# New order tables for an interleaved RWKV-6 attention and exact-GELU MLP

## The chip, the cores and the metric

The kernel runs on one core of one Trainium2 chip. The metric is the device time of one execution in microseconds, as the median of several runs. A profile is one further execution, recorded by the hardware profiler; its span is the time from its first to its last instruction.

## What is computed

An RWKV-6 attention with a recurrent state feeds an MLP with an exact GELU:

```python
# r, k, v, w: (4, 8, 768, 48), u: (8, 48)
for t in range(S):
    cur = einsum('bhd,bhe->bhde', u * k[t], v[t])
    y[t] = einsum('bhd,bhde->bhe', r[t], state + cur)
    state = w[t][..., None] * state + einsum('bhd,bhe->bhde', k[t], v[t])
x = y.transpose(0, 2, 1, 3).reshape(3072, 384)
h = x @ w_in                                   # (384, 2048)
g = 0.5 * h * (1.0 + erf(h / sqrt(2)))
out = g @ w_out                                # (2048, 384)
```

## The kernel before

The 3072 tokens are cut into 8 tiles of 384. For each tile there is an attention, `attention(x, unit)`, which leaves its result in `xT`, and an MLP, `mlp(x)`. Both are Python generators: each `next` emits the instructions of one small step. The instructions of an engine run in the order in which they are emitted, so the order of the steps is the schedule.

That order is written out by hand in two tables.

`PLAN[x]` has one character for each step of stage x. In stage 0 "." and "s" are the two units (halves of the heads) of the attention of tile 0, "l" a transfer of raw weights or of the second tile's data, "c" a step of the conversion of the weights, "f" a step of the next tile's attention, "w" the load of the next tile's v. In stages 1 to 7 "." is a step of the MLP of tile x - 1, "s" a step of the attention of tile x, "f" a step of the attention of tile x + 1, "l" a transfer for tile x + 1, "x" one of five sums of `xT` that the MLP needs (`sums_of_x`, L1029), "c" again the conversion (stage 1), "w" masks and sums of weights (stages 1 and 2). What is left of a stream when the characters end is emitted after them, save "f" (and "c" in stage 0), whose stream goes on in the next stage. The MLP of the last tile stands alone at the end.

`ORDER[x]` gives the steps of the MLP of tile x, for x from 1 on (tile 0 has a plain MLP: 16 blocks of 128 features, three products and a Gelu each, then the products with `w_out`). A letter and a digit is a step of the first half: capital letters A to G are products on TensorE, small letters mostly copies and Gelus on ScalarE. "+" is a sum on VectorE, "=" a product of the second half, "<" and "!" open and read out a bank of PSUM. The products use fewer multiplications than the plain form, with sums of blocks in their place.

The attention of tile 0 is the only work of stage 0. Each of its units makes diagonal products, then for six levels of block length a burst of products (L550), a scaling (L592, L603) and a copy by mask or by rows (L615, L612); then the transposed k (L787, L789), the state products (L817), the chain of states (L838, L833), the products with v (L859), fences that read the end of each bank (L869, L871), the products with the state (L906), and the copies into `xT` (L913, L929), part of it by way of `ysb` and transfers (L932, L936). Two warm-up matmuls (L324) stand behind most bursts. Loads in stage 0 are gated: a one-element memset on VectorE (L259, L303) stands ahead of each, so that the transfer can't be issued before VectorE has come to that place.

From tile 2 on, the attention has finer steps ("quarters": bursts L689 and L680, copies L723, L705 and L773, scalings L745, L752, L756, layouts L656, L662, L664). A weight arrives as 64-bit floats; three ScalarE operations (L432, L433, L435) and two VectorE operations (L440, L443) convert a piece of it.

Of the kernel before, what the change touches and what calls it, by code (L numbers as in the profile page):

```python
# [37 lines left out]
HALFWAY = 2  # L38
PLAN = {
    0: (  # L40
        "lllll.lll.lll.l.s.s.ssssss..sc.sssl.s.lcl.s.s.s.s..lcls.ssc.s.c.s.s.cs..cscss.s.sfwf."
    ),
    1: (
        "s.ccc.csc..cc.c.scc.scc....wscccc.c.ccsccs...cws.cccl.slclcs.cs..lslccc...ccsc...scccs.c...c.ccslwcc"
        "css..cslcc.csc.ccsccl.slc.sl...ccc.....w..f.....wfwf..wwwf..wf..xwf...wf.x.wff.f.x..ffxxw."
    ),
    2: (
        "w..s.s.slws.wws..wsw.ss.ss..s..ss.s.s.s...wl.ss......wss..s.s.sws..s.....s.ss.sws.ssw.sw..s.wss.sw.s"
        "ss.ss.w.ws.s.......s.l..ss.w....w....s.l..w.w.....sss.ll.....s....s.s...s..sss.ss.s.....ls......lls."
        ".......f.s.f..f.f....fxx....flx..x.x"  # L50
    ),
    3: (
        "s..s.............s.....s.s..ss..ss..sss..s...s.s...sssssss.s.s.l.....sssl.s..sss..s....s...ss...sss."
        ".s.sss.ss...s..s....l.....s.sls.s.....s.....s...s.ssss.s.s.l.slss....ss....s....l.ss....s.sl...lfs.."
        "...f.l....ffxx..xxx."
    ),
    4: (
        "......ss...s.......ll...s...s.s..l.......s..sls...ss.ss...s.sss.sss.sss..sss..s...s.s....ss.ssss...."
        ".ss..lss..s.sss...s...s.sl...ss..sss..s.ss.s..s.ss.......s.sss.s.s.s.........s.....s...l.ss.ls....l."
        "sfs...f..f.xxl...x.xx"  # L60
    ),
    5: (
        "s..s.s.......s..s..s....s.......s..s........sss..s...sss....sl.ss.sss.sssss....s...ss.sss...s....s.."
        "s.ls..sl.s.ss.s.s.s.s.s...s..s..s.s.s.sls.s.ssllsss.s.....sss.s..........s..s.........ss..s.llss..l."
        ".ss.f...f.f..fxx.xxl.fx."
    ),
    6: (
        "s..l...sl....s..ss................ss......sssls.s.....sl...sss.s.ssss.ss..s.s....ss...sss..ss...s..s"
        "....s...ss.s.ss.ssss.....l.ss....s..ss..s...s.s....s....sssss.sss.ss.....l......s.ss...ssls.l...l.fs"
        "..s.f...f..ff.xxf.xf.lfffffxx"  # L70
    ),
    7: (
        "........................ss.s...ss...s.ssss..s..ss.s..s......s...sss..ss....s..ss.ssss.s..ss..ssss..."
        ".s.s...ss...s.s..........s..s.s.ss.ss..s.s........s..s..s...ss.ss.s..ss.....ss.s.s......x.x...x..x.x"
    ),
}

# [19 lines left out]
W_ORDER = "empsiclratkdjfnbohqg"  # L97
ORDER = {
# [5 lines left out]
    ),  # L104
# [5 lines left out]
    ),  # L110
# [5 lines left out]
    ),  # L116
# [5 lines left out]
    ),  # L122
# [5 lines left out]
    ),  # L128
# [5 lines left out]
    ),  # L134
# [1187 lines left out]
```

## Time and profile before

| what | value |
|---|---|
| runs | 584.16, 584.63, 587.84 us; median 584.63 |
| the profiled execution, its own time | 587.29 us |
| its span | 585.5 us |
| TensorE (PE) busy | 566.6 us (97%) |
| VectorE (DVE) busy | 451.5 us (77%) |
| ScalarE (ACT) busy | 290.7 us (50%) |
| GpSimd (POOL) busy | 58.9 us (10%) |
| mean granted clock of TensorE | 0.997 |
| bytes moved | 55.07 MB, mean 94 GB/s |

How to read it: a row of the timeline has the start and length in us, the engine, the line of the kernel, the operation, what it writes and reads, how many instructions were merged, and in brackets how long the engine was idle before and what ended that. PEld is TensorE's loading of weights, which overlaps its products. SPq and ACTq are transfers issued by SyncE and ScalarE. The chain is the work that ended last, followed back step by step; "issue" in it, or in brackets, is time in which an engine waited for nothing that the profile shows. A product of 32-bit numbers leaves two records.

### The profile page before, as it was taken

To read this page: it belongs to the slowest core of one execution; us is meant where nothing else is said; L and a number is where in the kernel's file an instruction comes from. 1 tells how busy PE (TensorE), PEld (TensorE's weight loads), DVE (VectorE), ACT (ScalarE), POOL (GpSimd) and SP (SyncE) were. 2 spreads that over 40 slices of the span, in tenths; PEclk is the share of its full clock that TensorE was granted. 3 is DMA by queue.
4 is the path that set the end of the run, shared out by engine and by line. 5 is a ranking of instruction groups with operands and counts; after the bars stand their busy time and mean duration, and the time that the engine had idled before them with its cause. 6 is when DMAs were issued, how large, how long until landed. Compare 5 with 4: busy or idle time off the path is not lost.

```text
span 585.5 us, 17564 instructions
## 1 busy us (share of the span) xinstructions
PE 566.6 (97%) x7544; PEld 510.5 (87%) x7544; DVE 451.5 (77%) x880; ACT 290.7 (50%) x634; POOL 58.9 (10%) x63
## 2 busy tenths in 40 slices
PE   6879999999999999999999999989999999999997
PEld 3566667669999999999999999979999999999997
DVE  5879867998999977798897979789797988830171
ACT  2457997224852357335672367225571456525520
POOL 3100000003100111003100120002200031002200
PEclk9989999999999999999999999999999999999999
DMA  8538951123450523636222622525413242203401
GB/s 303 191 93 278 355 178 58 52 76 42 54 156 12 137 37 45 152 106 139 39 42 61 169 30 29 130 77 153 57 28 88 79 70 29 44 12 67 55 1 40
DMA packets 61853, 55.07 MB, mean 94 GB/s; under 512 B 32336, under 2 KB 46928, under 8 KB 61776
## 3 DMA queue, kind: packets, MB, share of 16 engines
q1 hardware_dynamic: 50256, 45.62, 25.5%
q0 software_dynamic: 11424, 8.26, 10.8%
q8 instruction: 59, 0.97, 0.7%
q14 instruction: 18, 0.15, 0.1%
q10 hardware_dynamic: 96, 0.07, 0.1%
HBM read 36.24 MB, written 4.72 MB: 70 GB/s over the span
## 4 chain that ended last, share of the span: by engine, by line
PE 90%; DVE 3%; issue 2%; DMA 2%; ACT 1%; SPq 1%; ACTq 0%; DVEq 0%
PE u_ps L1043 31%; PE h_ps L1043 19%; PE o_ps L1043 13%; PE h_ps L1121 5%; PE o_ps L1133 5%; PE d L689 5%; PE d L550 3%; PE y_ps L859 2%; PE y_ps L906 2%; PE kv_ps L817 2%; DMA xT<-ysb 1%; PE warm L324 1%; SPq L936 1%; DMA rkw<-in_rkw_dram 1%; DVE tot_sb L508 1%
## 5 line engine op out<-in xcount | busy, mean ns | idle before, releaser
L1043 PE MATMUL h_ps<-xT,w_in_sb 128*128 128x192 f32 x560 | 110.1, 329 | 1.4 <-DVE xT L1029 1.3
L1081 POOL DMA_DIRECT2D g<-o_sb x42 | 50.9, 1293 | 480.1 <-ACT o_sb L1076 336.4
L1043 PEld LDWEIGHTS h_ps<-xT,w_in_sb 128*128 128x128 f32 x560 | 93.2, 190 | 4.2 <-DVE xT L1029 1.9
L705 ACT COPY a_sb<-d 32x320 f32<-32x320 f32 (+5 forms) x108 | 39.1, 362 | 6.6 <-PE d L689 4.9
L1043 PE MATMUL u_ps<-s,w_in_sb 128*128 128x192 f32 x224 | 41.4, 328 | 0.0
L1043 PE MATMUL u_ps<-w_out_sb,g 128*128 128x192 f32 x224 | 41.3, 328 | 0.0
L1043 PE MATMUL o_ps<-t,g 128*128 128x192 f32 x224 | 40.6, 327 | 0.0
L1043 PEld LDWEIGHTS o_ps<-t,g 128*128 128x128 f32 x224 | 36.9, 190 | 0.5 <-ACT o_sb L1076 0.3
L1043 PEld LDWEIGHTS u_ps<-s,w_in_sb 128*128 128x128 f32 x224 | 36.9, 190 | 0.5
L1043 PEld LDWEIGHTS u_ps<-w_out_sb,g 128*128 128x128 f32 x224 | 36.9, 190 | 0.3
L723 DVE COPY_PREDICATED a_sb<-quarter,d 128x480 f32<-128x480 uint8 (+5 forms) x54 | 23.1, 438 | 12.9 <-PE d L689 11.7
L1121 PE MATMUL h_ps<-xT,w_in_sb 128*128 128x384 f32 x96 | 32.3, 491 | 0.3 <-ACT xT L913 0.3
L1133 PE MATMUL o_ps<-w_out_sb,g 128*128 128x384 f32 x96 | 32.4, 491 | 0.0
L1091 ACT COPY u_ps<-h_ps 128x384 f32<-128x384 f32 x28 | 13.1, 467 | 36.5 <-PE h_ps L1043 36.1
L550 PEld LDWEIGHTS d<-rkw 64*64 64x64 f32 x1152 | 19.6, 136 | 13.1 <-issue 7.5
L1043 PE MATMUL u_ps<-w_extra,g 128*128 128x192 f32 x168 | 30.7, 327 | 0.3 <-ACT u_ps L1167 0.3
L833 DVE SCALAR_TENSOR_TENSOR st<-st,tot_sb,kv_ps 128x48 f32<-128x48 f32 x160 | 29.4, 257 | 1.4 <-PE kv_ps L817 1.3
L932 ACT COPY ysb<-y_ps 128x384 f32<-128x384 f32 x8 | 3.8, 480 | 53.7 <-PE y_ps L906 42.9
L1072 ACT ACTIVATE g<-g 128x384 f32<-128x384 f32 x56 | 28.4, 522 | 3.6 <-DMA g<-o_sb 2.5
L689 PE MATMUL d<-kx,rkw 64*64 64x96 f32 x1152 | 29.4, 247 | 0.0
L1188 ACT ACTIVATE o_sb<-u_ps 128x192 f32<-128x192 f32 x21 | 6.9, 330 | 45.2 <-PE u_ps L1043 45.0
L1083 DVE TENSOR_TENSOR g<-g,o_sb 128x384 f32<-128x384 f32 x14 | 7.6, 554 | 28.0 <-ACT o_sb L1076 28.0
(163 smaller groups left out, 1234.5 us busy)
## 6 DMA issues: line engine op xcount, KB each, us to landing
rkw<-in_rkw_dram SPq DMA_DIRECT2D x54, 256.0 KB, 3.5
g<-o_sb POOLq DMA_DIRECT2D x42, 192.0 KB, 3.6
raw<-in_w_out_dram SPq DMA_DIRECT2D x8, 768.0 KB, 6.1
v_in<-in_v_dram SPq DMA_DIRECT2D x8, 584.0 KB, 3.9
raw<-in_w_in_dram SPq DMA_DIRECT2D x5, 768.0 KB, 8.3
rkw<-kx SPq DMA_DIRECT2D x72, 48.0 KB, 2.0
out_dram<-o_sb SPq DMA_DIRECT2D x17, 192.0 KB, 1.9
rkw<-in_rkw_dram SPq DMA_DIRECT2D x6, 384.0 KB, 6.7
```

Of the source, the lines that this page charges most:

```text
L550: nc.tensor.matmul(d[half[p], g, n * width:(n + 1) * width], lhsT=kc[half[g], b, i, p], rhs=right(half[g], b, i, p), start=True, stop=True)
L689: nc.tensor.matmul(o[half[p], i * 3 * C // 2:(i + 1) * 3 * C // 2], lhsT=kc[half[g], n // NI, n % NI, p], rhs=rx[half[g], 2 * n + p], star ...
L705: nc.scalar.copy(out=at[z, g, first:behind, (a + 1) * h:], in_=d[z, :, :, to] if g == slice(None) else d[z, :, to])
L723: nc.vector.copy_predicated(out=an[:, :, :, :, (a + 1) * h:], mask=mask.to_broadcast(data.shape), data=data)
L817: nc.tensor.matmul(kv_ps[half[g], p, i * D:(i + 1) * D], lhsT=k_t(b, i, p, g), rhs=vs(b, i, g)[half[p], 0:D], start=True, stop=True)
L833: nc.vector.scalar_tensor_tensor(out=stq[:, q, c], in0=stq[:, q, c - 1] if c else b4[:, q, NC - 1], scalar=totq[:, q, c:c + 1], in1=kvs[q ...
L1043: nc.tensor.matmul(o, lhsT=lhsT, rhs=rhs, start=start, stop=True, skip_group_check=True)
L1072: nc.scalar.activation(out=g_of(q, a, b), in_=z, func=AF.Gelu)
L1081: nc.gpsimd.dma_start(out=o, in_=z, accum_op=ALU.add)
L1091: nc.scalar.copy(out=u_of[q], in_=a_of[q])
L1121: nc.tensor.matmul(h_ps, lhsT=w_in_sb[:, f // FI, j, f % FI * 128:(f % FI + 1) * 128], rhs=xT[:, j, :], start=(j == 0), stop=(j == NJ - 1))
L1133: nc.tensor.matmul(o, lhsT=gs[f // FG][:, f % FG, i * 128:(i + 1) * 128], rhs=w_out_sb[:, f, :], start=(f == 0), stop=(f == NF - 1))
```

## The change

Only the two tables change. The table of stage 0 is replaced by one with the same steps in another order (the order that it had in the kernel ahead of the finer attention steps). The tables of stages 1 to 7, and the orders of the MLPs of tiles 1 to 6, are replaced by new ones; that of the MLP of tile 7 stays. The instructions are the same ones, and the numbers of steps of the next tile's attention that stand in a stage ("f") change from 12, 6, 4, 3, 5, 12 to 17, 9, 3, 3, 4, 12 in stages 1 to 6. The core of it, in which "..." marks what is left out:

```diff
 PLAN = {
     0: (
-        "lllll.lll.lll.l.s.s.ssssss..sc.sssl.s.lcl.s.s.s.s..lcls.ssc.s.c.s.s.cs..cscss.s.sfwf."
+        ".lls.....sslsc.lsslll.sl.sls..sl.lscsl..sss.lscs.lscs.s.clll.s..s.cccsss...wss..ss.ff"
     ),
     1: (
-        "s.ccc.csc..cc.c.scc.scc....wscccc.c.ccsccs...cws.cccl.slclcs.cs..lslccc...ccsc...scccs.c...c.ccslwcc"
-        "css..cslcc.csc.ccsccl.slc.sl...ccc.....w..f.....wfwf..wwwf..wf..xwf...wf.x.wff.f.x..ffxxw."
+        "c.ccc.clccs.cc..csscc...wcsc.csc.s.c.ccsc.scl..c..csclwccs.ccc.sc.cccs..ccs.c..csss.c...s.ccss.scl.l"
+        "wccc..ll.csccl.ccclcc.cfc.cwfwf..wcw.sfff...ff.w....lww.fff.fsfx.xfx..w.w.....w.f..f.cw.f..xx.."
     ),
     2: (
-        "w..s.s.slws.wws..wsw.ss.ss..s..ss.s.s.s...wl.ss......wss..s.s.sws..s.....s.ss.sws.ssw.sw..s.wss.sw.s"
-        "ss.ss.w.ws.s.......s.l..ss.w....w....s.l..w.w.....sss.ll.....s....s.s...s..sss.ss.s.....ls......lls."
-        ".......f.s.f..f.f....fxx....flx..x.x"
+        "ss.w.s.sswssw.s.s....s...slsl.s.s.sw..ww.ss.w..sw...sw.ss..w......swws.ss..s.s..s.sss.l.wsw..s..ss.."
+        ".s..l....ls.w..sw..s...w.s....ss.ssww.s..w.s...s.s.s..s.sl.s.......s.s.l........s..ls.s......s...l.."
+        "f...ls...f..ff....fx.xx....ff.xffx"
     ),
...
     5: (
-        "s..s.s.......s..s..s....s.......s..s........sss..s...sss....sl.ss.sss.sssss....s...ss.sss...s....s.."
-        "s.ls..sl.s.ss.s.s.s.s.s...s..s..s.s.s.sls.s.ssllsss.s.....sss.s..........s..s.........ss..s.llss..l."
-        ".ss.f...f.f..fxx.xxl.fx."
+        "...ss..ss.s..ss....s..s................l..ss.l.....s.slss.ss...s.ss.s....ss.s..s...sssss.sss..ss..s."
+        "s....s...ssss.sss..s...ssss....s....ssss...s....sls.sssss..s..s........l.....s.....s..ssls..sl..ls.l"
+        ".sf....f.f.f...lxxxx.x."
     ),
     6: (
-        "s..l...sl....s..ss................ss......sssls.s.....sl...sss.s.ssss.ss..s.s....ss...sss..ss...s..s"
-        "....s...ss.s.ss.ssss.....l.ss....s..ss..s...s.s....s....sssss.sss.ss.....l......s.ss...ssls.l...l.fs"
-        "..s.f...f..ff.xxf.xf.lfffffxx"
+        "...s...s.s.ss.s...s............l.s.....s...ss...ss....s.ss.s..ss..ssslss...s.s...ss.s.s...l.s.sl..ss"
+        "s.s...s.s.ss..ss.s.s.sss..s.s...ss..s.ssss..sss...l..s...s.s..ss.s..........s....sl......ss.ls.l.lfs"
+        ".s.ff.f....f..l..xx.xfffffffxx"
     ),
...
 ORDER = {
     1: (
-        "A0 a0 E0 e0 F0 B0 C0 b0 f0 A1 G0 c0 a1 E1 g0 B1 e1 F1 k0 f1 D0 b1 G1 A2 l0 C1 g1 d0 a2 j0 B2 c1 l1 E2 F2 "
-        "e2 b2 i0 k1 A3 f2 j1 C2 D1 c2 d1 G2 a3 g2 E3 F3 D2 e3 d2 l2 f3 i1 B3 b3 C3 k2 G3 <i c3 g3 k3 l3 =a i2 i3 "
-        "D3 j2 +01 d3 <g j3 =i +00 !b =b +23 =g +03 !a =k +22 +e0 +e5 +e1 !g +e2 +e3 =j +E2 !j +E3 !k =h !h =c =m "
-        "!c +20 !m +e4 =q !q =l <p =n !n !i +E0 +E4 !l =s !s =o =p !p =f =t !f !o =r !t !r =d =e !e !d"
+        "E0 e0 A0 a0 C0 c0 F0 B0 A1 b0 a1 E1 B1 F1 f0 e1 f1 k0 G0 G1 b1 g0 D0 A2 d0 a2 C1 l0 B2 g1 i0 c1 E2 e2 F2 "
+        "C2 D1 j0 b2 l1 c2 d1 A3 k1 f2 G2 a3 g2 j1 k2 l2 i1 E3 e3 F3 f3 D2 C3 +22 c3 G3 g3 B3 =a +e5 D3 d2 <i l3 "
+        "b3 d3 <g j3 j2 k3 i2 i3 +23 +03 +e0 =i =b +e1 =g =j +01 +e2 =k !b !k !g +e3 !a +E2 +E3 =h !j =c =m !h "
+        "+00 =q !m +20 !c <p +E0 +e4 !q =l +E4 =n !l !n =s =p =o !s !p =f =t !f !o =r !t =d =e !r !d !i !e"
     ),
...
     4: (
-        "A0 E0 a0 e0 B0 F0 b0 C0 f0 A1 G0 c0 k0 a1 F1 g0 E1 B1 f1 D0 b1 e1 d0 G1 A2 C1 l0 a2 g1 B2 c1 F2 b2 E2 i0 "
-        "A3 e2 k1 D1 d1 C2 a3 l1 j1 f2 j0 G2 c2 k2 g2 F3 E3 e3 i1 f3 B3 D2 C3 c3 l2 d2 i2 G3 j2 +22 g3 b3 =a k3 "
-        "D3 l3 +e5 <i i3 +e2 d3 !a j3 +03 +23 =b +01 <g =g +e0 =k +e1 =i =j !g +e3 =c !k !j =h +E3 !d +E2 !h +00 "
-        "+20 =m !i =q !m !q +e4 =l +E4 !l =n +E0 =s !c !s <p !n =p =f !p !f =o =t !o !b !t =r !r =d =e !e"
+        "A0 E0 a0 B0 e0 F0 b0 C0 f0 A1 G0 c0 E1 k0 a1 B1 g0 F1 e1 D0 b1 A2 l0 f1 C1 G1 d0 a2 g1 l1 B2 c1 b2 E2 D1 "
+        "e2 F2 A3 f2 C2 j0 j1 d1 c2 a3 k1 k2 G2 F3 g2 i0 E3 f3 D2 i2 B3 e3 G3 l2 i1 g3 D3 d2 C3 b3 +22 <i l3 +e5 "
+        "j2 j3 +e2 c3 d3 =i <g =b +03 +23 =g =a =k k3 !g =j +e0 i3 =h !d !k !j +01 !a =c +e1 +E2 +e3 +E3 !i +00 "
+        "!h =m +20 !c !m +e4 =q <p !q =l +E0 !l +E4 =p =n =s !n !p !s =o !o !b =f =d !f =t =r !t !r =e !e"
     ),
     5: (
-        "A0 a0 E0 e0 B0 F0 b0 C0 f0 A1 G0 a1 c0 g0 F1 f1 l0 B1 E1 b1 e1 D0 d0 j0 k0 A2 C1 G1 a2 B2 c1 g1 E2 b2 F2 "
-        "D1 l1 f2 d1 e2 k1 j1 C2 c2 A3 a3 G2 i1 F3 !b g2 E3 k2 D2 f3 e3 G3 i0 i2 l2 C3 g3 +22 j2 c3 !a D3 B3 k3 "
-        "+e5 l3 d2 b3 <i d3 !i =a <g j3 i3 +23 =i +03 +01 +e1 =b +e2 +e0 +00 =j +e3 =g +E3 !j =k +20 !g =c +E2 !k "
-        "=h !h =m =q +e4 !m =l +E0 !c !q =n !l !d <p +E4 !n =o =s !s =p !p =f =t !f =r !o !t =d !r =e !e"
+        "A0 E0 a0 F0 e0 B0 C0 b0 A1 f0 a1 G0 F1 g0 l0 f1 B1 c0 E1 e1 G1 b1 D0 C1 g1 k0 d0 A2 a2 c1 D1 !b E2 d1 B2 "
+        "b2 l1 i0 F2 e2 C2 j0 k1 i1 c2 f2 A3 a3 G2 k2 F3 E3 g2 f3 D2 G3 d2 e3 l2 g3 j1 C3 i2 c3 B3 D3 +22 <i l3 "
+        "!i k3 d3 =b <g j3 j2 +03 =g b3 +23 =i +e0 i3 !a =a +e5 +01 !g =k =h =j +e1 !k !j +e3 !h =c +e2 +E3 +E2 "
+        "=m =q !c +00 !m !d +20 !q =l <p +e4 !l +E0 =p =n +E4 !p =s !n =o !s !o =t =f !f =d !t =r =e !r !e"
     ),
...
```

More of the change, by code (lines that the diff above doesn't have):

```diff
@@ L52 @@
-    3: (
-        "s..s.............s.....s.s..ss..ss..sss..s...s.s...sssssss.s.s.l.....sssl.s..sss..s....s...ss...sss."
-        ".s.sss.ss...s..s....l.....s.sls.s.....s.....s...s.ssss.s.s.l.slss....ss....s....l.ss....s.sl...lfs.."
-        "...f.l....ffxx..xxx."
-    ),
-    4: (
-        "......ss...s.......ll...s...s.s..l.......s..sls...ss.ss...s.sss.sss.sss..sss..s...s.s....ss.ssss...."
-        ".ss..lss..s.sss...s...s.sl...ss..sss..s.ss.s..s.ss.......s.sss.s.s.s.........s.....s...l.ss.ls....l."
-        "sfs...f..f.xxl...x.xx"
-    ),
@@ L72 @@
-    7: (
-        "........................ss.s...ss...s.ssss..s..ss.s..s......s...sss..ss....s..ss.ssss.s..ss..ssss..."
-        ".s.s...ss...s.s..........s..s.s.ss.ss..s.s........s..s..s...ss.ss.s..ss.....ss.s.s......x.x...x..x.x"
+        "c.ccc.clccs.cc..csscc...wcsc.csc.s.c.ccsc.scl..c..csclwccs.ccc.sc.cccs..ccs.c..csss.c...s.ccss.scl.l"
+        "wccc..ll.csccl.ccclcc.cfc.cwfwf..wcw.sfff...ff.w....lww.fff.fsfx.xfx..w.w.....w.f..f.cw.f..xx.."
+    ),
+    2: (
+        "ss.w.s.sswssw.s.s....s...slsl.s.s.sw..ww.ss.w..sw...sw.ss..w......swws.ss..s.s..s.sss.l.wsw..s..ss.."
+        ".s..l....ls.w..sw..s...w.s....ss.ssww.s..w.s...s.s.s..s.sl.s.......s.s.l........s..ls.s......s...l.."
+        "f...ls...f..ff....fx.xx....ff.xffx"
+    ),
@@ new lines @@
+    3: (
+        ".................l...l...ss..s..ss...s.lsss..s..sss.s.s.sss..s..s.s.s......s.ss.ss.ss..s..ss.sss..ss"
+        ".ss.s....l.sl..ss.....s.......ss.s.s..ss..s.s.ss..s.s...s......s.s...l....ssss..l..s.s.l..s.ls.f...f"
+        "......lfxx.xx..x"
+    ),
+    4: (
+        ".s.ss.l.......s.s............s....sl..s....sssss..s.ss..ss..s..ss......s.s..ssss..ss.sl..s..s..s.s.s"
+        "s.s.....s.ss.ssss..ss.s.lss..ss.s..s.....s.s.l.s.s......sss.....ss.....ss..s...s.ssl..s..s...llsls.f"
+        "....s.....f.l..fxx.xxx"
+    ),
@@ L75 @@
+    7: (
+        "........................s.s....sssss.s......sss.ss...ss.s...ssss..ss..s.s...ss.ss.....s..s.ss.s..s.s"
+        "ss.s...s....s..s......s.s......s.....s..ss.ssss..s.ssss...s........s..s.s.s.s.s....s.......xx....xxx"
     ),
```

24 rows, old and new, of the table ORDER are left out of this document.

## The prediction

> **What bounds the kernel now.** I read the page first, then a table of busy time by stage, then the timeline and the chain of the first 60 us, and last the rows of the later stages in which TensorE (PE) waits. The page says that PE is the engine that is full:
>
> ```profile
> span 585.5 us, 17564 instructions
> PE 566.6 (97%) x7544; PEld 510.5 (87%) x7544; DVE 451.5 (77%) x880; ACT 290.7 (50%) x634; POOL 58.9 (10%) x63
> ```
>
> The table by stage has the stretch, its length, then each engine's busy time and count, the granted clock, DMA share and rate. Its rows are the head (attention of tile 0), the last 3 us before the MLP of tile 0, that MLP, and six stages with one MLP and one attention each:
>
> ```profile
> 0.00:46.00 46.00, 34.81 (x1095) 24.54 (x1096) 34.30 (x105) 18.78 (x30) 7.98 (x21) 0.96 0.56 188
> 46.00:49.10 3.10, 2.84 (x101) 1.92 (x98) 2.87 (x9) 2.99 (x7) 0.00 (x0) 1.00 0.59 158
> 49.10:127.00 77.90, 77.72 (x973) 49.12 (x974) 65.96 (x105) 51.57 (x72) 0.00 (x0) 1.00 0.49 171
> 127.00:193.00 66.00, 66.00 (x834) 63.13 (x833) 60.35 (x114) 33.10 (x81) 7.37 (x6) 1.00 0.34 70
> 193.00:260.00 67.00, 67.00 (x856) 64.37 (x855) 53.43 (x105) 33.19 (x81) 7.27 (x6) 1.00 0.41 92
> 260.00:328.00 68.00, 67.83 (x846) 65.52 (x847) 58.35 (x112) 34.16 (x83) 7.26 (x6) 1.00 0.38 85
> 328.00:394.00 66.00, 63.92 (x836) 61.36 (x834) 54.83 (x101) 31.94 (x79) 7.27 (x6) 1.00 0.35 79
> 394.00:460.00 66.00, 65.83 (x832) 63.23 (x832) 57.33 (x106) 33.28 (x81) 7.27 (x6) 1.00 0.36 78
> 460.00:526.00 66.00, 65.14 (x844) 62.90 (x845) 47.18 (x94) 32.39 (x80) 7.24 (x6) 1.00 0.26 49
> 526.00:585.50 59.50, 55.52 (x338) 54.41 (x336) 16.94 (x37) 19.35 (x45) 7.20 (x6) 1.00 0.21 40
> ```
>
> From 49.10 on the clock is 1.00 and PE is full but for 0.18 us in the first MLP, 0.17 + 2.08 + 0.17 + 0.86 = 3.28 us in the six stages and 3.98 us in the last one. The change removes and adds no matmul, so the time can move only by (a) when the first MLP starts, (b) PE work that moves across that start, (c) PE's waits after it, and (d) how often PE goes from MLP to attention and back. The table of the last MLP is unchanged, so its 59.50 us stay.
>
> **Head, early part: nothing, between -0.8 and +1.4 us.** The new order sends the weight pieces and the second tile's data later and brings unit 1's chain of decay products ahead of unit 0's first scalings.
>
> ```profile
> 10.29 0.55 DVE L508 TENSOR_TENSOR tot_sb<-rkw 128x384 f32<-128x384 f32 x1
> 11.58 0.93 PE L550 MATMUL d<-rkw 64*64 64x64 f32 x48 [0.64 <-DMA rkw<-in_rkw_dram]
> 19.26 1.37 issue
> 39.27 1.40 PE L859 MATMUL y_ps<-a_sb,v_in 64*64 64x64 f32 x57 [2.94 <-issue]
> ```
>
> VectorE does these products (the row shows the first of six) in either place, and unit 1's matmuls wait for their own data until 11.58 anyway. From there to 32 us PE's bursts and VectorE's updates alternate; the number of bursts, their sizes and their warm-up matmuls are the same, in nearly the same sequence. PE's stops called "issue" (1.37 and 2.94 us in these rows) come at the same instruction counts. If the first of these stops goes because the queue is emptier, VectorE, which has two conversion steps to do there, gives back all but about 0.8 us; if another stop of its size is added, 1.37 is lost. I take nothing.
>
> [...]
>
> **Head, late part: -2.0 us, between -2.8 and 0.** Before, the first step of the next attention stands on ScalarE (ACT) ahead of unit 0's copies into xT:
>
> ```profile
> 42.84 0.48 ACT L932 COPY ysb<-y_ps 128x384 f32<-128x384 f32 x1 [4.81 <-PE y_ps L906]
> 43.35 2.68 ACTq L936 DMA_DIRECT2D xT<-ysb  x3
> 46.08 2.13 ACT L497 ACTIVATE kx<-rkw,u_sb 128x384 f32<-128x384 f32 x4 [2.76 <-DMA xT<-ysb]
> 46.84 2.00 PE L550 MATMUL d<-kx,rkw 64*64 64x64 f32 x96
> 48.12 0.94 ACT L913 COPY xT<-y_ps 48x384 f32<-48x384 f32 x2
> 49.11 8.01 PE L1121 MATMUL h_ps<-xT,w_in_sb 128*128 128x384 f32 x24 [0.27 <-ACT xT L913]
> ```
>
> The new order ends "..ss.ff": the copies L913 go ahead of the four L497. They start at about 46.05 and end at 47.0, and the MLP starts at 47.1 in place of 49.11. A gain is lost only if the last of the three transfers that ACT issues until 46.03 lands much later. The v load moves ahead of the three transfers on SP's queue; it waits for unit 0's matmuls with v, which end about 40.7, and so is issued ahead of the 43.3 at which these are wanted.
>
> **Work that moves across the start: +1.6 us (1.5 to 2.0).** The 96 diagonal matmuls (46.84) ran in front of the MLP, in time that PE had free. Now they come after the first block of 128 features, in time that it has not. Paced by PE a burst of 96 takes 1.53 in the chain below; the 2.00 above was paced by the L497 beside it.
>
> **A new wait in the first MLP: +1.3 us (0 to 2.0).** ACT converts weights (three operations, L432, L433, L435) and applies Gelu (L1124) in order. Before, two Gelus follow the first conversion; now there is a conversion between them.
>
> ```profile
> 49.08 0.93 ACT L432 ACTIVATE f<-raw 128x768 f32<-128x768 f32 x1
> 52.07 0.49 ACT L1124 ACTIVATE g<-h_ps 128x384 f32<-128x384 f32 x1
> 53.28 0.49 ACT L1124 ACTIVATE g<-h_ps 128x384 f32<-128x384 f32 x1 [0.72 <-PE h_ps L1121]
> 53.91 0.92 ACT L432 ACTIVATE f<-raw 128x768 f32<-128x768 f32 x1
> 56.69 0.46 ACT L1124 ACTIVATE g<-h_ps 128x384 f32<-128x384 f32 x1
> 57.12 1.53 PE d L550 x96
> ```
>
> A conversion takes 52.07 - 49.08 = 2.99 us or 56.69 - 53.91 = 2.78. Counted from the MLP's start: L497 until 2.0, conversion until 5.0, first Gelu 5.5, conversion 8.4, second Gelu 8.9. PE (8.01 for four blocks, so 2.0 each) does block 0 until 2.0, the diagonal until 3.6, block 1 until 5.6, block 2 until 7.6. Block 3 needs the bank that the second Gelu frees, at 8.9: 1.3 us of waiting. Behind block 3 on PE stands the next attention burst, and VectorE, ACT and later bursts wait for that one; each of them comes late by the same 1.3, not by more, since the blocks after it find their Gelus done by the same count. At the end of that phase ACT copies the transposed k only after one more Gelu and two more copies, and the state matmuls wait for it: +0.3 (0 to 1). Where all of this is hidden, it costs nothing, and I keep 0 as the lower end.
>
> **Later stages: -2.5 + 0.4 + 1.3 us.** The waits of before that I can name:
>
> ```profile
> 378.28 3.24 DVE L833 SCALAR_TENSOR_TENSOR st<-st,tot_sb,kv_ps 128x48 f32<-128x48 f32 x18 [0.29 <-PE kv_ps L817]
> 381.31 1.63 PE L859 MATMUL y_ps<-a_sb,v_in 64*64 64x64 f32 x96 [0.33 <-DVE st L833]
> 383.23 0.57 PE L906 MATMUL y_ps<-rkw,st 64*64 64x64 f32 x22 [0.17 <-DVE fence L871]
> 385.12 1.27 PE L906 MATMUL y_ps<-rkw,st 64*64 64x64 f32 x70 [1.32 <-issue]
> 460.86 2.22 PE L1043 MATMUL h_ps<-xT,w_in_sb 128*128 128x192 f32 x12 [0.98 <-DVE xT L1029]
> 209.05 1.50 PE h_ps L1043 x8
> 213.65 1.30 PE h_ps L1043 x8
> ```
>
> In the stage 328 to 394 the two y bursts stand next to each other, and PE waits 0.17 for the fence and 1.32 for instructions between them. The new tables put a product of 1.3 us between these bursts in every stage: -1.5. The 0.33 stays, since there are again two products (2.6) beside a chain of state updates of 3.24. In the stage that ends at 460 four products stand behind the last attention burst, and the MLP then waits 0.98 for sums of x; the new table has five there: -1.0. Each return to the MLP costs 1.50 - 1.30 = 0.2 us, and counting the bursts in both tables I find 50 returns before and 52 after: +0.4. New waits in six new tables I can't read off. Before, they had 3.28 us in all; the two that I remove make 2.5 of it. I take 1.3, four tenths of 3.28; the bounds are 0 and 3.3.
>
> **Sum, on the profiled execution:** -2.0 + 1.6 + 1.3 + 0.3 - 2.5 + 0.4 + 1.3 = +0.4, a span of 585.9 for 585.5. That execution's own time was 587.29, 2.66 above the median 584.63 of the runs; the same offset gives 585.0 us. A measurement of this kernel tells about 1% (5.8 us) from no change, so this is no change.
>
> **Rivals.**
>
> 1. *The gains come without the waits*: ACT's waits are hidden (-1.6), an instruction stop shortens (-0.8), the new tables have no waits of their own (-1.3). +0.4 - 3.7 = -3.3, so 581.3. For it: PE has 0.18 us of waits in the whole first MLP now, so Gelus were well placed. Against it: the count above by blocks. Beyond -5.8 nothing is to be had: all waits of the six stages are 3.28.
> 2. *Slower: VectorE (DVE) bounds the second tile's stage.* Its row (127 to 193) has 60.35 of 66 us, free 5.65. The new orders move two layout steps out and three steps of the third tile's attention (a scaling with its products, and two sums) in, which the second tile's rows price:
>
> ```profile
> 116.67 0.90 DVE L516 TENSOR_TENSOR rkw<-rkw 128x384 f32<-128x384 f32 x1
> 117.61 0.86 DVE L480 TENSOR_TENSOR kx<-rkw,rkw 128x384 f32<-128x384 f32 x1
> 118.65 2.70 DVE L473 TRANSPOSE_TENSOR_REDUCE rkw<-kx 128x36 f32<-128x1152 f32 x3
> 127.10 0.55 DVE L662 TENSOR_TENSOR kx<-rkw,tot_sb 128x384 f32<-128x384 f32 x1
> 129.53 0.96 DVE L664 TENSOR_TENSOR kx<-kx,tot_sb 128x768 f32<-128x768 f32 x1 [0.53 <-ACT kx L656]
> ```
>
> Out go 0.55 + 0.96, in come 0.90 + 0.86 + two thirds of 2.70 = 3.56, so 62.4. The other five stages leave DVE 13.6, 9.7, 11.2, 8.7 and 18.8 us idle because it waits for PE and ACT. From 3.6 us of such waits on, PE waits; at 10.8, the mean of the first four, it is 62.4 + 10.8 - 66 = +7.2: 592.2. For it: that row is the fullest. Against it: before it managed with 5.65.
> 3. *The earlier start doesn't come*: the transfers land late, or the stops of PE grow with the later weight loads, which now meet the fetches at 30 to 37 us. Then the -2.0 is 0 and the rest stays: +2.4, so 587.0.
>
> **How the numbers follow.** Forecast 0.52, rival 1 0.20, rival 2 0.13, rival 3 0.15. The likeliest gives 585.0. Rival 1 sets the low end with half a microsecond for its own doubt (580.8); the high end (590.8) takes in rival 3 with the upper bound of new waits (587.0 + 2.0) and the wait of block 3 and the diagonal at their upper ends, and leaves most of rival 2 out. Faster by over 1% (under 578.8) needs more than all waits: 0.03. Slower by over 1% (over 590.5) is rival 2 and a little of rival 3: 0.15. Within 1%: 0.82.
>
> **What would show it.** Right: L913 ahead of L497 on ACT and the first L1121 near 47; the 96 diagonal matmuls behind the first block of the MLP; a wait for ACT L1124 of about 1.3 us in front of the fourth block; no "issue" above 1 us between the y bursts; no wait for L1029 near 1 us. Wrong: a stage of the six with more than 3 us of PE idle, DVE above 64 of 66 us in the second tile's stage, a first MLP that starts at 49 or later, or one that is 79 us long without a wait for ACT.

## The result and the profile after

| what | before | after |
|---|---|---|
| median, beside each other | 585.79 us (14 runs) | 583.13 us (14 runs) |
| ratio | | 0.9951, 95% interval 0.9932 to 0.9970 |
| profiled execution: its own time, span | 587.29, 585.5 us | 583.43, 581.7 us |

The changed kernel ran twice more beside other versions: ratio 0.9927 (0.9904 to 0.9950) and 0.9932 (0.9907 to 0.9957). It is 0.5 to 0.7% faster: by 2.7 us in the first comparison, where the prediction had +0.4 us, no change. The page of the profile after, first two lines, and its table by stage (stretch, length, busy time and count of PE, PEld, DVE, ACT and POOL, granted clock, DMA share, GB/s):

```profile
span 581.7 us, 17597 instructions
PE 567.2 (98%) x7544; PEld 510.4 (88%) x7544; DVE 453.0 (78%) x880; ACT 290.2 (50%) x634; POOL 58.8 (10%) x63
```

```profile
0.00:46.00 46.00, 36.27 (x1098) 24.90 (x1099) 35.63 (x107) 20.41 (x34) 7.97 (x21) 0.96 0.66 206
...
46.10:125.80 79.70, 79.70 (x1075) 50.36 (x1073) 68.51 (x111) 54.62 (x79) 0.00 (x0) 1.00 0.47 163
125.80:191.50 65.70, 65.70 (x834) 63.46 (x834) 58.95 (x112) 32.11 (x78) 7.37 (x6) 1.00 0.37 79
191.50:257.90 66.40, 66.24 (x851) 63.67 (x849) 54.12 (x102) 33.07 (x80) 7.23 (x6) 1.00 0.37 84
257.90:323.60 65.70, 65.70 (x834) 63.27 (x834) 56.18 (x105) 32.80 (x80) 7.23 (x6) 1.00 0.37 77
323.60:389.50 65.90, 65.18 (x841) 62.30 (x841) 56.12 (x106) 32.93 (x80) 7.23 (x6) 1.00 0.37 84
389.50:455.60 66.10, 66.05 (x836) 63.55 (x835) 58.03 (x108) 32.52 (x80) 7.24 (x6) 1.00 0.38 85
455.60:522.00 66.40, 66.40 (x853) 63.96 (x852) 48.95 (x99) 32.40 (x80) 7.28 (x6) 1.00 0.26 49
522.00:581.70 59.70, 55.83 (x340) 54.81 (x338) 16.44 (x34) 19.22 (x45) 7.23 (x6) 1.00 0.21 40
```

PE's idle time in the six stages is 0.16 + 0.72 + 0.05 = 0.93 us, after 3.28. The eleven profiles of other runs with the new tables have 0.8 to 1.4 there; e1 and e3 below, with the old ones, have 3.2 and 2.1. In the two profiled spans the first MLP starts 3.02 us earlier, the stretch from there to the pair of L208 matmuls behind it is 1.35 longer (79.15 after 77.80), and all that comes behind this pair is 2.20 shorter (456.41 after 458.61). The timeline around the first MLP (start, length, engine, line, operation, idle time before and its end):

```profile
41.36 0.48 ACT L932 COPY ysb<-y_ps 128x384 f32<-128x384 f32 x1 [0.26 <-PE y_ps L906]
41.87 2.17 ACTq L936 DMA_DIRECT2D xT<-ysb  x3
44.14 0.96 ACT L913 COPY xT<-y_ps 48x384 f32<-48x384 f32 x2 [2.30 <-DMA xT<-ysb]
44.79 1.47 PE L324 MATMUL warm<-zeros 128*128 128x512 bf16 x6
45.12 2.13 ACT L497 ACTIVATE kx<-rkw,u_sb 128x384 f32<-128x384 f32 x4
46.09 2.10 PE L1121 MATMUL h_ps<-xT,w_in_sb 128*128 128x384 f32 x6
46.44 1.14 PEld L1121 LDWEIGHTS h_ps<-xT,w_in_sb 128*128 128x128 f32 x4 [0.15 <-DMA xT<-ysb]
48.12 1.63 PE L550 MATMUL d<-kx,rkw 64*64 64x64 f32 x96
49.68 6.34 PE L1121 MATMUL h_ps<-xT,w_in_sb 128*128 128x384 f32 x18
53.30 0.46 ACT L1124 ACTIVATE g<-h_ps 128x384 f32<-128x384 f32 x1
```

L913 now stands ahead of L497, the MLP starts at 46.09 in place of 49.11, and the 96 diagonal products follow its first block. Inside the row of 6.34 there is a wait for the Gelu of about 0.3 (18 products take 6.0 to 6.1 without one).

### The profile page after: what moved, and what is told of

Read it like the earlier page. It is cut to its first block, busy times and chain, and to the rows that moved or that the text cites. A ratio compares the mean times of both kernels' runs of the same rounds, so it can differ in the third digit from the quotient of the medians.

```text
span 581.7 us, 17597 instructions
## 1 busy us (share of the span) xinstructions
PE 567.2 (98%) x7544; PEld 510.4 (88%) x7544; DVE 453.0 (78%) x880; ACT 290.2 (50%) x634; POOL 58.8 (10%) x63
## 4 chain that ended last, share of the span: by engine, by line
PE 94%; DVE 2%; DMA 1%; issue 1%; ACT 0%; SPq 0%; DVEq 0%
PE u_ps L1043 33%; PE h_ps L1043 19%; PE o_ps L1043 13%; PE h_ps L1121 6%; PE o_ps L1133 5%; PE d L689 5%; PE d L550 4%; PE kv_ps L817 2%; PE y_ps L906 2%; PE y_ps L859 2%; DMA rkw<-in_rkw_dram 1%; PE warm L324 1%; DVE st L833 1%; PE d L680 1%; DVE kx L487 1%
## 5 line engine op out<-in xcount | busy, mean ns | idle before, releaser
L550 PEld LDWEIGHTS d<-rkw 64*64 64x64 f32 x1152 | 20.2, 140 | 12.9 <-issue 8.3
L1157 DVE TENSOR_TENSOR g<-g 128x512 f32<-128x512 f32 x42 | 28.1, 682 | 3.4 <-ACT g L1072 3.1
```

The source lines that it names most:

```text
L550: nc.tensor.matmul(d[half[p], g, n * width:(n + 1) * width], lhsT=kc[half[g], b, i, p], rhs=right(half[g], b, i, p), start=True, stop=True)
L1157: (nc.vector.tensor_add if op == "+" else nc.vector.tensor_sub)(*(a(i) for i in (z if z != "E0" else "20", x_, y_)))
```

## Where the first 46 us go: instruction blocks and the clock

Two things in the trace vary from one execution to the next. PE stops without a wait that the profile shows ("issue": 2.94 us ahead of 39.27 before, 1.21 ahead of 25.04 after; that it stops for instructions is shown below, with e14), and its granted clock falls to 0.50 for 3.4 us after some of these stops. Clock rows of the kernel before and of the changed one, a microsecond each (length, PE busy and count, granted clock, DMA share, GB/s):

```profile
37.00:38.00 1.00, 0.00 (x0) 1.00 0.13 49
...
39.00:40.00 1.00, 0.73 (x41) 0.89 0.00 0
40.00:41.00 1.00, 1.00 (x39) 0.50 0.06 16
...
43.00:44.00 1.00, 1.00 (x75) 0.90 0.07 16
```

```profile
24.00:25.00 1.00, 0.00 (x0) 1.00 0.87 180
25.00:26.00 1.00, 0.96 (x35) 1.00 0.48 187
26.00:27.00 1.00, 0.49 (x9) 0.89 0.11 28
27.00:28.00 1.00, 1.00 (x44) 0.50 0.00 0
...
30.00:31.00 1.00, 1.00 (x34) 0.91 0.65 94
```

Before, half the clock follows the stop of 2.94 us; after, it follows a stop of 1.21 and a wait of 0.51 for VectorE (L603), within 3.4 us in which PE was busy for half of the time. The same stop does not always do it: e3 below, with the old start, had this stop at 2.67 us and the full clock throughout. The clock records of before's and after's traces have two values, 1.00 and 0.50. In all 20 traces the clock changes at whole multiples of 3.413 us: before's stands at 1.00 for 34.133 us (10 of them), at 0.50 for 3.413 and at 1.00 for 542.719 (159). This grid starts at another time in each execution: the half clock begins at 39.78 in before's and at 26.77 in after's, 2.23 and 2.88 us behind a multiple of 3.413. What goes with the change is the share of a window in which PE is busy. Cut at this grid, the 20 traces have 3348 windows at the full clock. Each of the 20 in which PE was busy for less than 41% of the time was followed by half the clock, 6 of the 17 between 41 and 51% were, and none of the 3311 above. So here it mattered how a stop lay to the grid. The 2.94 of before lies in one window (36.37 to 39.78, PE busy for 15%); the 2.67 of e3 is shared by two (33.25 to 40.08, 56% and 65%), and nothing follows.

An episode shows in a run's mean clock as 0.997 in place of 1.000. Over the timed runs, the mean clock is 0.999 or more in 15 of 121 with the old start of stage 0 and in 44 of 77 with the new one (a version of the new start with early loads, 1 of 6, and the one with a much later MLP, 0 of 7, not counted). Fitted over all runs, 0.001 of mean clock is worth 0.32 us (0.25 to 0.39). The last stop ahead of the products with the state (L906; 2.94 in before's profile, 1.44 in after's) has a mean of 2.76 us over nine profiles with the old start (1.57 to 3.49), and of 1.61 over eleven with the new one (0.61 to 2.67).

## The experiments

**One part at a time.** Four versions on one chip:

```diff
 e1: before, with the table of stage 0 of after
 e2: after, with the table of stage 0 of before
 e3: before, with only the end of that table changed, diagonal products behind the first block
-  s.sfwf.    next: s.ccc
+  s.s.ffw    next: .sccc
 e4: after, with the loads of stage 0 early, as before
```

> The kernel before with the new table of stage 0 alone; the 96 diagonal matmuls still stand in front of the first MLP, as in the table of stage 1 before. Theory A (the gain has two parts, about 1.2 us from the head and 1.5 to 2.3 us from the tables of the later stages): the first MLP starts 1 to 1.5 us earlier than before, and the median is 1 to 1.5 us below before. Theory B (all of it comes from the later tables; what the head gains is paid back by the diagonal matmuls): 0 to 0.5 us below. Theory C (all from the head): 2.5 us below.

> The kernel after with the table of stage 0 as before; all later tables are the new ones, so the diagonal matmuls stand behind the first block of the MLP, and the copies into xT behind the four scalings, as before. Theory A: 0.5 to 1.5 us below before, since the diagonal matmuls now cost 1.6 us and the later stages give 2.3 back. Theory B: 2.5 us below. Theory C: within 0.5 us of before or slower by up to 1.

> The kernel before with two moves only: unit 0's copies into xT go ahead of the four scalings, and the diagonal matmuls behind the first block of the MLP. By the prediction's step (start 2.0 us earlier, 1.6 us of diagonal matmuls inside the MLP, no new wait for a Gelu, since the two first Gelus stay together): 0.4 us below before, and the first MLP starts near 47.1. If the start is bounded by the landing of the last transfer into xT: start at 48 or later, and 0.5 us or more above before.

> The kernel after with the transfers of weights and of the second tile's data as early as before (eleven of the seventeen at their places in the table before, the last five as after). Theory A with the landing of unit 0's data as the cause of the earlier first burst (7.80 after, 8.77 before): first burst again at 8.7, unit 1's k a microsecond later, and 0.5 to 1 us above after. If the early landing is eaten up later in the head by PE's stops for instructions: first burst at 8.7, the same time as after within 0.3 us.

| version | median, us | ratio to before (95%) |
|---|---|---|
| e1, new stage 0 alone | 584.58 | 0.9979 (0.9964 to 0.9993) |
| e2, new later tables alone | 584.60 | 0.9976 (0.9963 to 0.9989) |
| e3, copies L913 first, diagonal products moved | 584.54 | 0.9980 (0.9964 to 0.9995) |
| e4, after with early loads | 583.27 | 0.9957 (0.9941 to 0.9973) |

e1 and e2 give about 1.3 us each, and both together are the 2.7 of the change: they add. e3, with only the end of the new stage 0, gives as much as e1. Loading late or early is worth nothing that can be measured. The later e5 and e10 take the start and the swap of the copies apart on top of the new tables:

```diff
 e5: after, with stage 0 of e3
 e10: after, with L497 and the first products ahead of L913 again
-  ..ss.ff
+  ..ssff.
```

> The changed kernel, but the table of stage 0 is the old one with the copies L913 ahead of the four L497. Theory A (all of the head's gain lies in that one swap, the other reordering of stage 0 gives nothing): the same time as the changed kernel, ratio to before 0.9955 (583.2 us), within 0.6 us. Rival B (the early part of the new stage 0 gives some of it, through fewer instruction stops or a full clock): 0.6 to 1.2 us slower than the changed kernel, ratio 0.9965 to 0.9975.

> The changed kernel with one thing undone: the four L497 and the first products of the second tile stand ahead of unit 0's copies L913 again. Theory A (that swap is worth what it gave on the kernel before, 1.3 us): ratio to before 0.9973, 1.3 us slower than the changed kernel, first MLP at about 48. Rival B (on top of the new start it is worth little, because the landing of the transfers sets the start anyway, as the run without warm-ups showed): within 0.5 us of the changed kernel.

> The changed kernel itself once more, on the same chip as the two versions of it that run beside it: ratio to before 0.995 as in its first runs, and its granted clock at full in about half of the executions.

e5: 584.97 us, 0.9975 (0.9952 to 0.9998). e10: 583.90, 0.9965 (0.9941 to 0.9988), beside e12, the changed kernel again, 582.41, 0.9927. So the swap is worth about 1.5 here (0.3 to 2.5, from resampling the executions of e10 and e12), and the old start costs as much or more, by which the theory behind e5 (all of the head's gain lies in the swap) falls. I fitted one number for each of three parts to all runs of before, after and e1, e2, e3, e5, e10, with a level for each group of runs made side by side: **early part of stage 0 -0.9 (+-0.7), copies first -0.9 (+-0.6), later tables -1.2 us (+-0.5)**. With the mean clock in the fit as well, the early part falls to -0.3 (+-0.6), so most of it goes with the clock.

The fit doesn't place these parts in the kernel, since the move of the 96 diagonal products comes with the later tables in e2, with the copies in e3 and not at all in e1. The traces do. From the copy L932 to the end of the MLP's first four blocks they show 14.5 us with the old end of stage 0 (mean of six profiles, 14.1 to 15.0), 14.8 with the changed one (nine, 14.4 to 15.5), 14.4 with the copies first and the diagonal products still ahead (e1), and 15.6 and 15.5 with the copies last and the diagonal products behind the first block (e2, e10). So the copies in front save about 0.8 only where the diagonal products have been moved, and the two moves together save nothing in this stretch. The fit counts the cost of that move among the later tables, which is why they give it 1.2 where the profiles show 2.2 behind the first MLP. The 1.3 of e3 isn't in its stretch (14.5) and stays unexplained.

e10's trace shows what the swap does beside letting L913 go first. The second tile's first products now run into the end of an instruction block, a stop that the changed kernel has not:

```profile
42.64 1.17 PE L550 MATMUL d<-rkw 64*64 64x32 f32 x65 [1.36 <-issue]
```

**Where the stops come from.**

```diff
 e14:
-    keep_warm(16)
+    keep_warm(24)
```

> The changed kernel with 24 warm-up matmuls in place of 16 at the very start, eight more instructions of TensorE (and eight weight loads) ahead of everything else. Theory A (the stops called issue stand where the next block of 128 matmuls with their weight loads has to be fetched: the trace's instruction queue moves 59 packets of 16 KB for 7544 matmuls): the bursts are cut eight matmuls earlier, 15/33 becomes 7/41, and the last stop ahead of the chain of states, with 10 of 48 state products (L817) left, comes with 18 left. Rival B (the stops come from the load of the transfer queues at a time): the cuts stay at the same matmul or vanish.

PE rows of the changed kernel, and of e14:

```profile
23.37 0.45 PE L550 MATMUL d<-rkw 64*64 64x64 f32 x15
25.04 0.73 PE L550 MATMUL d<-rkw 64*64 64x64 f32 x33 [1.21 <-issue]
...
36.92 0.74 PE L817 MATMUL kv_ps<-v_in,kx 64*64 64x48 f32 x38
39.10 0.37 PE L817 MATMUL kv_ps<-v_in,kx 64*64 64x48 f32 x10 [1.44 <-issue]
```

```profile
22.71 0.34 PE L550 MATMUL d<-rkw 64*64 64x64 f32 x7
24.26 0.85 PE L550 MATMUL d<-rkw 64*64 64x64 f32 x41 [1.21 <-issue]
...
36.37 0.63 PE L817 MATMUL kv_ps<-v_in,kx 64*64 64x48 f32 x30
38.03 0.49 PE L817 MATMUL kv_ps<-v_in,kx 64*64 64x48 f32 x18 [1.04 <-issue]
```

Eight matmuls more in front, and the cuts come exactly eight earlier: 15/33 is 7/41, 38/10 is 30/18. In the changed kernel's profile the first three stops stand ahead of the 222nd, 350th and 478th matmul, 128 apart. The stops stand at counts of instructions, and the page tells of which size:

```profile
q8 instruction: 59, 0.97, 0.7%
```

59 packets of 16.4 KB for 7544 matmuls and as many weight loads is one for 128 matmuls. In the traces of before and after each of the eight stops called issue of 0.87 us or more ends 1.33 to 1.47 us behind the end of one of these packets (37.93 and 39.27 before, 37.69 and 39.10 after); in the head before, packets start at 30.04 and 36.98, among others. Over the profiles the stops at these places take 0.28 (e14) to 3.49 us (e6), where bursts of small matmuls use up 128 in 2.2 us (an estimate: 96 of L550 take 1.63).

Is their place worth time? e17 is e14 timed, beside the changed kernel (e18).

> The changed kernel with 24 warm-up matmuls in place of 16 at the start, now timed. Theory A (the sum of the stops is what counts, and moving all cuts by eight changes it by chance only: 0.54 + 0.28 + 1.21 + 1.04 = 3.07 us in its profile after 0.95 + 0.91 + 1.21 + 1.44 = 4.51): up to 1 us faster than the changed kernel beside it, more executions at full clock. Rival B (the single execution was a lucky one): the same within 0.6 us.

> The changed kernel beside it on the same chip: ratio to before 0.9945, between its two earlier results.

583.01 us, 0.9951 (0.9924 to 0.9979), beside 581.89, 0.9932: no gain. The profile of e18 has the first MLP at 43.47, where the earlier two of the same kernel have 46.09 and 45.06. One profile of the head is off by more than any term that I summed there.

**What the start of the MLP waits for.** e7 leaves the last six warm-ups out (`range(2)` to `range(0)` in the step that calls L324).

> The changed kernel without the six warm-up matmuls (L324) that stand last in stage 0, right ahead of the first MLP (1.47 us in the profile). Theory A: they cost nothing, because the first MLP's third weight load waits until the last transfer of ysb into xT has landed (46.44) and because ACT's conversions set when block 3 can run: the same time within 0.4 us. Rival B: the MLP starts up to 1.0 us earlier and the time falls by that, to a ratio of 0.9935 to before.

```profile
46.45 2.17 PE L1121 MATMUL h_ps<-xT,w_in_sb 128*128 128x384 f32 x6 [0.84 <-DMA xT<-ysb]
```

583.35 us, 0.9941 (0.9912 to 0.9970), the changed kernel's time: the warm-ups fill a wait for the transfers of ysb. Two versions tried to use that wait for the diagonal products:

```diff
 e8: L497 as a step of its own, ahead of L932, third conversion behind L913, no last warm-ups
-  s.cccsss...wss..ss.ff    next: c.ccc.clccs.cc..c
+  s.sss...fwss..ss.cccff   next: sc....cccclcc.ccc
 e9: after, no last warm-ups, four of the six transfers on SyncE
-  c.ccc.clccs.cc..c
+  sc.ccc.cl..cc.ccc
```

> A version that should beat both: the changed kernel with the four L497 ahead of the copy L932 (they may run as soon as the state products have read the transposed k, about 39.5), the third conversion behind the copies L913, the 96 diagonal products ahead of the first MLP, in the time in which TensorE waits for the transfers into xT, two Gelus ahead of the next conversion, and without the six last warm-ups. Theory A: first MLP at 46.4 with the diagonal products done, and no wait for a Gelu in front of the fourth block: 1.3 us less than the changed kernel, ratio to before 0.993 (581.8 us). Rival B (the L497 delay the copy L932 and with it the transfers by their own 2.1 us): MLP start at 48, no gain. Rival C (VectorE or ACT is late later on in the first MLP, since one conversion stands later): the first MLP grows by what the start gains.

> Second attempt at a version that beats both: the changed kernel, in which SyncE issues four of the six transfers of ysb into xT and ScalarE two (before, three each), the 96 diagonal products stand ahead of the first MLP's first block, the second Gelu ahead of the next conversion, and the last six warm-ups are left out. The order of conversions on VectorE stays. Theory A (what is late ahead of the MLP is the chain copy L932, issue, landing, and ACT's L913 and L497 behind its issues): ACT is free 0.7 us earlier, L497 end at 46.5, the diagonal products are done at 46.6 and the MLP starts there, which is 1.1 us less than 46.09 with 1.63 of diagonal products to come; no wait for a Gelu (0.3): ratio to before 0.993, 1.0 to 1.4 us less than the changed kernel. Rival B: the fourth issue on SyncE delays the last landing by as much (0.6), and the raw weights behind it, so the gain is half a microsecond or nothing.

e8: 591.02 us, 1.0062 (1.0039 to 1.0084). Its trace shows two waits that I had not seen coming:

```profile
43.38 3.43 ACTq L938 DMA_DIRECT2D xT<-ysb  x3
45.95 1.11 SPq L299 DMA_DIRECT2D raw<-in_w_in_dram  x2
51.54 6.69 PE L1123 MATMUL h_ps<-xT,w_in_sb 128*128 128x384 f32 x20 [1.77 <-DMA xT<-ysb]
62.38 1.77 PE L552 MATMUL d<-rkw 64*64 64x32 f32 x96 [4.15 <-DVE a_sb L617]
```

The small transfers that ScalarE issues until 46.81 land at 51.5, almost 5 us later, with SyncE's raw weights issued from 45.95 on beside them (whether these delay them was not tried); and the moved conversions hold up VectorE's queue until the attention's next burst waits 4.15. e9 (584.25, 0.9968, 0.9947 to 0.9989) avoids both and still loses to the changed kernel:

```profile
45.86 1.38 PE L550 MATMUL d<-kx,rkw 64*64 64x64 f32 x75 [1.36 <-issue]
47.16 8.01 PE L1121 MATMUL h_ps<-xT,w_in_sb 128*128 128x384 f32 x24
```

With the diagonal products ahead of the MLP, the end of an instruction block falls 21 matmuls into them and costs 1.36. Behind the MLP's first block, as in the changed kernel, no stop shows in them. So e9's start is 47.16, not the 46.6 I expected. No version was shown to beat the changed kernel.

How long the MLP then waits for a Gelu depends on how far ScalarE is ahead of it. In the changed kernel's rows above, L497 begins 0.97 us before the MLP and the wait is 0.3. In e4 and e17 the copies L913 end later than the warm-ups, so that L497 and the MLP both begin behind them, within 0.03 of each other, and the wait is 0.84 and 0.88. The rows of e4:

```profile
45.88 2.13 ACT L497 ACTIVATE kx<-rkw,u_sb 128x384 f32<-128x384 f32 x4
45.91 2.20 PE L1121 MATMUL h_ps<-xT,w_in_sb 128*128 128x384 f32 x6 [0.26 <-ACT xT L913]
...
54.58 2.20 PE L1121 MATMUL h_ps<-xT,w_in_sb 128*128 128x384 f32 x6 [0.84 <-ACT g L1124]
```

**The wait for L1029 and the y bursts.** e6 makes by hand the two edits that the prediction counted on, in the old tables; the four after it ask what removes the wait in front of the seventh tile's MLP.

```diff
 e6, stage 5: a product between the y bursts
-  ss.
+  s.s
 e6, stage 6: y bursts one product earlier (e13, e15: this too)
-  .fs..s.
+  s.f.s..
 e11 and e13, end of stage 6
-  .ff.xx
+  .xxff.
 e15 and e16, end of stage 6
-  .ff.xx
+  ..xxff
```

> The kernel before with two places changed: in stage 5 one product of the MLP is put between the two y bursts (L859, L906), in stage 6 both y bursts come one product earlier, so that five products stand behind them. Only these two stages of the profile are read. The prediction's terms: stage from 328 to 394 1.5 us shorter than the 67.98 of before's profile (66.5), stage from 394 to 460 (and the wait for L1029 at its end) 1.0 shorter. Rival, after the results: the stop of 1.32 between the y bursts is one for instructions that comes and goes between executions (the run with the old tables behind the new copies had that stage at 66.43 without any edit), so the first gain is 0 to 0.3 against that run, while the second is there in full, since it is a wait for VectorE.

> The kernel before with one change in stage 6: the first two sums of x (L1029) stand ahead of two steps of the next attention on VectorE (L508 and the 2.18 us L480) instead of behind them. Only the end of that stage is read. The run with one more product of the MLP behind the y bursts did not shorten the wait for L1029 (1.39 after 0.98), so the prediction's reason for the gain of 1.0, five products in place of four, is in doubt. Theory A (VectorE's order sets it): the wait of 0.98 goes to below 0.2 and stage 6 ends about 0.9 earlier. Rival B (the sums wait for the transfers into xT, or the copies of the attention): the wait stays.

> The kernel before with both moves in stage 6: the y bursts one product earlier, so that five products stand behind them, and the first two sums of x (L1029) ahead of two steps of the next attention on VectorE. Only the end of that stage is read. Alone, the first left a wait of 1.39 (the sums stood behind the 2.18 us L480 until 460.1), the second one of 3.41 (VectorE waited 2.39 for the transfers of ysb, which landed at 459.1). Theory A (two causes, one behind the other: the transfers must land earlier and VectorE must be free): the transfers land about 1.5 us earlier, near 457.5, the sums follow, and the wait of TensorE in front of the next MLP goes to below 0.3. Rival B (the sums depend on something else that is late): it stays above 0.9.

> The kernel before with, in stage 6, the y bursts one product earlier (five products behind them) and the read-out (L1190) and the first two sums (L1029) ahead of the two steps L508 and L480 of the next attention. Only the end of that stage is read. Theory A (VectorE's 2.18 us step L480 in front of what the MLP needs is the cause): the transfers land at about 456.3, as with both moves, the sums follow, the read-out waits for its product only, and TensorE's wait goes below 0.4. Rival B (the wait only goes to the next item of VectorE's queue): over 0.9.

> The same without the first move: four products behind the y bursts, read-out and first two sums ahead of L508 and L480. The transfers land at 459.1 as in the run with the sums ahead, the second sum ends at 459.9, and TensorE's products end at 459.9. Theory A: the wait falls from 0.98 to 0.1 to 0.4, so the order on VectorE is the cause, and the fifth product is worth at most the rest. Rival B (five products are needed): it stays at 0.9 or more.

PE's waits at that place in e6, e11, e13, e15 and e16, one profile and one fence each:

```profile
447.36 1.63 PE L859 MATMUL y_ps<-a_sb,v_in 64*64 64x64 f32 x96 [0.85 <-DVE st L833]
...
460.91 2.22 PE L1043 MATMUL h_ps<-xT,w_in_sb 128*128 128x192 f32 x12 [1.39 <-DVE xT L1029]
```

```profile
463.45 4.21 PE L1043 MATMUL h_ps<-xT,w_in_sb 128*128 128x192 f32 x12 [3.41 <-DVE o_sb L1190]
```

```profile
460.63 3.90 PE L1043 MATMUL h_ps<-xT,w_in_sb 128*128 128x192 f32 x12 [2.03 <-DVE o_sb L1190]
```

```profile
464.00 0.92 PE L1043 MATMUL u_ps<-s 128*128 128x192 f32 x4 [0.82 <-DVE s L1029]
```

```profile
462.14 0.92 PE L1043 MATMUL u_ps<-s 128*128 128x192 f32 x4 [2.32 <-DVE s L1029]
```

Five products alone leave the wait (1.39) and add one of 0.85 for the chain of states. The sums ahead alone make it 3.41, and both together 2.03, because the read-out L1190 still stands behind VectorE's 2.2 us step L480. With the read-out ahead too, the wait in front of the MLP is gone, and the next sum is late by 0.82 or 2.32. Each move hands the wait on to the next item of VectorE's queue. The two stages around that place take 133.1 us before and 134.3 to 138.2 in these five; in e11 the wait is followed by 6.83 us of half the clock (the 12 products behind it take 4.21 us, in e6 2.22). The changed kernel has no such wait (131.7 us), nor has any other profile with the new tables more than 0.2 in that stage. Its order brings that step earlier, so that it is done before the sums' turn; no run takes this apart from the rest of the new order:

```profile
453.44 2.20 DVE L480 TENSOR_TENSOR kx<-rkw 128x1152 f32<-128x1152 f32 x1
...
456.26 0.36 DVE L1029 TENSOR_TENSOR s<-xT 128x192 f32<-128x192 f32 x1
```

As to the y bursts, e6's stage 5 is 66.29 us after 67.98, the predicted 1.5 and a little more. But e3, with the old table there, had the bursts without a stop and that stage at 66.43:

```profile
380.57 1.61 PE L906 MATMUL y_ps<-rkw,st 64*64 64x64 f32 x92 [0.17 <-DVE fence L871]
```

In other executions of the old table the stop was 1.32, 1.05, 0.73 or nothing.

## Why the prediction was wrong

The steps that failed are three terms of the sum: the new waits of the later tables and of the first MLP, put at 1.3 each, and the early head, put at nothing.

- **Early head, 0: wrong.** It measured -0.9 (+-0.7). The prediction saw that stops come at instruction counts, and took them as a cost of their own. It took their lengths from one profile, while the last of them is 1.15 us shorter on average with the new order, and did not see that the clock can stand at 0.50 for 3.4 us behind such a stop, as it did behind the 2.94 of before's profile.
- **Late head, -2.0: right in its mechanism, too large by half a microsecond.** L913 went first and the start moved by 3.02 in the profiles, but 1.48 of that is there at L932 already (42.84 to 41.36), which leaves 1.54. The profiled execution of before had its half clock right there, at 40 to 43; e2 and e3, with the same order up to that place and the full clock, have L932 at 40.43 and 40.09.
- **Diagonal products, +1.6: right**, 49.68 - 48.12 = 1.56.
- **Wait for the Gelu, +1.3: wrong, 0.3** (0.35 and 0.40 in the two other profiles of the changed kernel). The count began L497 and the MLP at the same time. In the trace L497 begins at 45.12 and the MLP at 46.09, because it waits for the transfers and stands behind six warm-ups, so ACT is a microsecond ahead. Where the two did begin together (e4, e17) the wait was 0.84 and 0.88. So the head start took off half a microsecond, and the count by blocks was 0.4 too long besides. The +0.3 behind it didn't come: the first MLP's stretch without the diagonal products is 77.43 in e1, and 77.43 + 1.56 + 0.27 = 79.26 leaves nothing of the 79.15. In all the late head had +1.2 in the sum, and the traces show about +0.2 (14.8 after 14.5).
- **Later tables, -1.5 - 1.0 + 0.4 + 1.3 = -0.8: too small a gain**, -2.2 in the two profiles (and -1.2 +-0.5 in the fit, which counts the moved diagonal products here). The mis-sized term is the new waits: 0.93 us of idle time in all is left, of which 3.28 - 2.5 = 0.78 were to stay, so 0.15 in place of 1.3. The -1.0 came, but not by five products alone, as e6 shows; the traces point to VectorE's order. The -1.5 is a stop that isn't in every execution; between these two profiles it came, and PE's idle time in that stage fell from 2.08 to 0.72.
- **The level.** The median of three runs, 584.63, was low: 585.79 over 14. The forecast of +0.4 on the span missed by 3 us in the difference. A difference under 1% was taken for none, while 14 executions of each kernel give an interval 0.4% wide.
- Rival 1 (581.3, the gains without the waits) was the nearest in the difference, -3.3 beside the measured -2.7: of its three reductions, 1.6, 0.8 and 1.3, the waits in the first MLP gave 1.3, the early head 0.9, and the new waits 1.15. Against it stood only my count by blocks. Rivals 2 and 3 are out: VectorE had 58.95 of 65.70 us in the second tile's stage, and the earlier start came.

That the forecast of 585.0 misses the measured time by only 1.9, and not by the 3 of the difference, is luck: the level and the gain were both too low.

What stays open: why the last stop is shorter with the new start, where e3's 1.3 comes from, and how much of the early part is the stop itself and how much the clock behind it (beside the clock the fit leaves -0.3 +-0.6). Early loads had 2.42 us there and one full clock in 6 runs, a hint at the transfers beside the fetch, but too little to tell.

## What to carry to other kernels

A wait that a count of one engine's queue predicts is only paid if the other engine arrives on time: take its start from what bounds it last, here transfers that land. Moving an instruction out of a wait is no gain until everything that stands behind it in that queue has been followed as well; three moves in a row only handed the wait on. Where bursts of small matmuls run, see where the stops fall: here they stood 128 matmuls apart, with one packet of 16.4 KB of instructions for so many, and in the diagonal products one cost 1.36 ahead of the first MLP (e9) and nothing behind its first block. Do not build a term on one profile of such a stretch: the same stop cost its own length in e3 (2.67 us, full clock), and in before's profile (2.94), by its place in the clock's window, 3.4 us of half the clock besides.

## What the hardware showed unexpectedly

The place of TensorE's instruction stops is exact to the matmul (15/33 to 7/41 for eight more in front), while their length is not: the same stop of the same kernel took 1.44, 1.62 and 0.61 us in three profiles. The clock changed on a grid of 3.413 us that started at another time in each execution: it fell to 0.50 behind all 20 windows with PE busy for less than 41%, and behind 6 of 17 with 41 to 51%, one of them in after's profile (23.36 to 26.77, PE busy for 1.74 of 3.41 us).
